# Pooled attention with a Strassen output product: when x is turned, which queue loads and stores, and which engine combines

## The chip, the cores and the metric

The kernel runs on one core of a Trainium2 chip. The metric is the device time of one execution in microseconds (us). A core has several engines that run side by side, each with its own instruction queue: TensorE (PE, matrix products), VectorE (DVE), ScalarE (ACT), GpSimd (POOL) and SyncE (SP), which here only issues transfers. Sixteen DMA engines move the data. A transfer is put on a queue by the engine that issues it: in the profile q1 is the queue of SP, q10 that of ACT, and q0 ("software_dynamic") that of POOL.

## The reference

Eight batches of eight heads, 576 queries each, head size 64; keys and values are pooled by eight to 72. The attention output, as a 4608 x 512 matrix x, goes through two products with a function between them.

```python
def _attn_ref(q, k, v):
    pool = 8
    k_p = k.reshape(B, H, S // pool, pool, D).mean(axis=3)
    v_p = v.reshape(B, H, S // pool, pool, D).mean(axis=3)
    scores = np.matmul(q, k_p.transpose(0, 1, 3, 2)) / np.sqrt(D)
    scores = scores - np.max(scores, axis=-1, keepdims=True)
    attn = np.exp(scores)
    attn = attn / (np.sum(attn, axis=-1, keepdims=True) + 1e-09)
    return np.matmul(attn, v_p)

x = attn_out.transpose(0, 2, 1, 3).reshape(4608, 512)
h = x @ w_in            # w_in  512 x 2048
g = h - np.tanh(h)
out = g @ w_out         # w_out 2048 x 512
```

## The kernel before

The two products are worked in nine groups of 512 tokens (`TG`, g = 0 to 8). A batch has 576 tokens, so the borders of batches and groups drift apart: group g + 1 needs only the first blocks of batch g + 1, and the rest of that batch is read by group g + 2. Group 0 and the attention of batches 0 and 1 are a start of their own. From g = 1 on the order is written out by hand (the schedule is manual: each engine runs its instructions in program order, and semaphores tie the engines together), and each group has two phases.

In the **h phase** (line 934 on) PE computes x @ w_in by `h_pair` and `h_one` (line 530, 62 to 64 matmuls with 512 columns), reading `xT`, a ring of three groups' columns. ACT takes tanh, DVE subtracts (L543, L548) and adds up the sums that Strassen's scheme needs (P at L551, Q at L556).

In the **output phase** (line 962 on) seven products of Strassen's scheme (L586, 16 matmuls of 256 columns each) stand in for the eight of a 2 x 2 block product. `after_product` combines them into O: L626 after product 1, then differences Dg (L561), L631 on GpSimd and L635 after products 2 and 3, L638 after 4, L640 after 5; ACT copies the last quarter at L983. Between the products stands the attention of the next batch nb = g + 1: scores (L349) in steps 0 to 4, and in steps 6, 7, 8, 9 and 11 the products with V, one block of 128 queries each (`av`, L396). A block has two halves; each is normalised by DVE with a reciprocal (L413) and a multiplication (L414) into `x_sb`, and the block is then turned into `xT` by a DMA transpose on SP's queue (L434; a block that crosses the ring's end takes two).

SP's queue in a group, in order: five or six transposes of x (L434), one of k (L332, from `kd`, which POOL makes), five of q (L205, from `q_bf`, which ACT casts in the first three steps of the h phase), then the nine loads of k, v and q of batch nn = g + 2 (L137, L146, L141, L170, L162).

POOL's queue in a group: L631, then pooling of k (L248, L253, L256) and v (L267 to L291) of batch nn, then `k_place` (L300 to L304, which needs the turned k), then the stores of the group before (L607, five to eight transfers).

After the last group's phase SP stores O (L603, eight transfers), two halves of the last product are copied out (L994) and stored on SP and ACT (L996).

```python
if by_dma:                                   # in av, after both halves
    nc.sync.dma_start_transpose(out=xT[...], in_=x_sb[...])
if nn is not None:                           # third step of the h phase
    load_k(nn); load_v(nn); load_q(nn)       # all on nc.sync
if u == 6 and nn is not None:
    pool_k(nn, nc.gpsimd)
    pool_v(nn, nc.gpsimd)
```

Of the kernel before, what the change touches and what calls it, by code (L numbers as in the profile page):

```python
# [8 lines left out]
FP32 = mybir.dt.float32  # L9
# [3 lines left out]
ALU = mybir.AluOpType  # L13
PSUM = bass.MemoryType.PSUM

B, H, S, D = 8, 8, 576, 64
# [10 lines left out]
TG = 512  # L27
# [15 lines left out]
def kernel(  # L43
# [89 lines left out]
            nc.vector.tensor_copy(out=out, in_=in_)  # L133
        evac_n[0] += 1

    def load_main(src, dst, b, t0, t1):
        return nc.sync.dma_start(out=dst[:, t0:t1, :], in_=src[b, 0:128, t0:t1, :])  # L137

    def load_left(src, dst, b, eng=nc.sync):
        return [  # L140
            eng.dma_start(out=dst[32 * t : 32 * t + LO, NM, :], in_=src[b, 128:PR, t, :])  # L141
            for t in range(NM)
        ]

    def load_dense(src, dst, b, eng=nc.sync):
        return eng.dma_start(  # L146
            out=dst[0 : NM * LO, NM, :], in_=src[b, 128:PR, :, :]
        )

    def load_k(b):  # L150
        return [
            load_main(k_pairs, k_raw[b % 2], b, 0, NM),
            load_dense(k_pairs, k_raw[b % 2], b),
        ]

    def load_v(b):
        return [load_main(v_pairs, v_raw[b % 2], b, 0, NM)] + load_left(
            v_pairs, v_raw[b % 2], b
        )

    def load_q_tail(b, t, eng):
# [1 line left out]
            out=t[:QT, :, R, :], in_=q[b, :, QA:S, :].rearrange("h p d -> p h d")  # L163
        )

    def load_q(b, tail=True):
        if b not in q_raws:
            q_raws[b] = raw.tile([128, H, R + 1, D], FP32, name="q_raw", tag="q_raw")
        t = q_raws[b]
        nc.sync.dma_start(  # L170
            out=t[:, :, 0:R, :], in_=q[b, :, 0:QA, :].rearrange("h (p j) d -> p h j d", j=R)
        )
        if tail:
            load_q_tail(b, t, nc.sync)

    qTs = {}
    kdups = {}
# [60 lines left out]
    def halves(n, b):  # L238
        return ((0, n),) if b < 2 else ((0, n // 2), (n // 2, n))

    def pool_k(b, eng, t0=0, t1=NT, mid=()):
        r = k_raw[b % 2].rearrange("p t (j d) -> p t j d", d=D)[:, t0:t1, :, :]
        if b not in kdups:
            kdups[b] = work.tile([128, NT, 2, D], BF16, name="kd", tag="kd")
        kd = kdups[b][:, t0:t1, :, :]
        n = t1 - t0
        for ta, tb in halves(n, b):
            first = eng.tensor_tensor(  # L248
                out=r[:, ta:tb, 0:4, :], in0=r[:, ta:tb, 0:4, :], in1=r[:, ta:tb, 4:8, :], op=ALU.add
            )  # L250
        for c in mid:
            load_w2(c)
        eng.tensor_tensor(  # L253
            out=r[:, :, 0:2, :], in0=r[:, :, 0:2, :], in1=r[:, :, 2:4, :], op=ALU.add
        )
        eng.tensor_tensor(  # L256
            out=kd,
            in0=r[:, :, 0:1, :].to_broadcast([128, n, 2, D]),
            in1=r[:, :, 1:2, :].to_broadcast([128, n, 2, D]),
            op=ALU.add,  # L260
        )
        return first
# [158 lines left out]
    def new_x():  # L421
        return work.tile([128, 2, 4, D], BF16, name="x_sb", tag="x_sb", bufs=5)

    def av(b, blk, alloc, by_dma):
        x_sb = new_x()
        for half in range(2):
            av_half(b, blk, half, x_sb, alloc)
        if by_dma:
            p0 = 0 if blk < 4 else 64
            pos = (b * S + blk * 128) % RING  # L430
            p1 = min(128, p0 + RING - pos)
            for r0, r1, c in ((p0, p1, pos), (p1, 128, 0)):
                if r1 > r0:
                    nc.sync.dma_start_transpose(  # L434
                        out=xT[:, :, c : c + r1 - r0],
                        in_=x_sb[r0:r1, :, :, :].rearrange("p a h d -> p (a h d)"),
                    )
        return x_sb

    def x_pe_transpose(b, blk, x_sb, fbs=(0, 4)):  # L440
        p0 = 0 if blk < 4 else 64
# [116 lines left out]
        )  # L558

    def sum_d(a, b):  # L560
        nc.vector.tensor_tensor(  # L561
            out=Dg[:, a:b, :, :],
            in0=Gt[:, a:b, :, 0:HT],
            in1=Gt[:, a:b, :, HT:TG],
            op=ALU.subtract,
        )
# [30 lines left out]
            return PS[:, 2:4, 0:HD]  # L597
        return PS[:, bk, :].rearrange("p (t n) -> p t n", t=2)

    def store(g, th, c0=0, c1=DM):  # L600
        for tt in range(2):
            for r0, r1, dst in out_segments(g * TG + th * HT + tt * 128, 128):
                nc.sync.dma_start(out=dst[:, c0:c1], in_=O[r0:r1, 2 * th + tt, c0:c1])  # L603

    def store_tile(g, tb):
        for r0, r1, dst in out_segments(g * TG + tb * 128, 128):
            nc.gpsimd.dma_start(out=dst, in_=O[r0:r1, tb, :])  # L607

    def sh(c, off):
        return slice(c.start + off, c.stop + off)  # L610
# [8 lines left out]
        (C1, lambda k, c: Dg[:, k, 1, c], w2s[:, 2, :, :]),  # L619
    ]  # L620

    def after_product(g, n):
        if n == 0:
            nc.scalar.copy(out=m4, in_=chain(g, C1))
        if n == 1:
            nc.vector.tensor_tensor(out=O[:, 2:4, 0:HD], in0=chain(g, C2), in1=m4, op=ALU.add)  # L626
            sum_d(0, 2)
            sum_d(2, 4)
        if n == 2:
            nc.scalar.copy(out=m45, in_=chain(g, C1))  # L630
            nc.gpsimd.tensor_tensor(out=m4, in0=O[:, 2:4, 0:HD], in1=m45, op=ALU.subtract)  # L631
            sum_d(4, 6)
            sum_d(6, 8)
        if n == 3:
            nc.vector.tensor_tensor(out=O[:, 0:2, HD:DM], in0=m4, in1=chain(g, C2), op=ALU.subtract)  # L635
        if n == 4:
            nc.scalar.copy(out=m451, in_=chain(g, C1))  # L637
            nc.vector.tensor_tensor(out=m451, in0=m451, in1=m45, op=ALU.subtract)  # L638
        if n == 5:
            nc.vector.tensor_tensor(  # L640
                out=O[:, 2:4, HD:DM], in0=m451, in1=chain(g, C2), op=ALU.subtract
            )
# [288 lines left out]
    for g in range(1, NG):  # L931
        nb = g + 1 if g + 1 < B else None
        nn = g + 2 if g + 2 < B else None
        for p in range(NP - 1):
            c = p if g > 1 else p - 1
            if nb is not None and 0 <= c < 3:
                q_cast_part(nb, c)
            h_pair(g, p, (0, 2, 4, 6, 0, 2, 4)[p], p % 2)
            if g == 1 and p < 4:
                w_sum(w2s[:, 0, :, :], b11, b22, ALU.add, k0=2 * p, k1=2 * p + 2)  # L940
            if 3 <= p < 6:
                sum_p(2 * p - 6, 2 * p - 4)
            if nb is not None and p == 0:
                k_dma_transpose(nb)
                k_place(nb, nc.gpsimd.tensor_copy)
            if g > 1 and p == 0:
                for tb in range(4):
                    store_tile(g - 1, tb)
            if nb is not None and 0 <= c < 3:
                q_dma_transpose(nb, 2 * c, min(2 * c + 2, R + 1))  # L950
            if nb is not None and c == 2:
                if nn is not None:
                    load_k(nn)
                    load_v(nn)
                    load_q(nn)
        h_one(g, NP - 1, 1, 0, 2)
        h_one(g, NP - 1, 0, 1, 3)
        sum_p(6, 8)
        sum_q(0, 4)
        sum_q(4, 8)  # L960
        ps_a = Banks(2, 3, 4, 5, 0, 1)
        for u in range(14):
            n, half = u // 2, u % 2
            bk, lhs, rhs = products[n]
            if n == 6 and g == NG - 1:
                break
            product(g, bk, lhs, rhs, 4 * half, 4 * half + 4, n < 2)
            if half:
                after_product(g, n)
                if g == 1 and n in (1, 2):  # L970
                    w_sum(w2s[:, 2, :, :], b21, b22, ALU.add, k0=4 * n - 4, k1=4 * n)
            if nb is not None:
                if u < NT:
                    scores(nb, u)
                if u == NT:
                    ps_a.n += 2
                if u in (6, 7, 8, 9, 11):
                    av(nb, (6, 7, 8, 9, 11).index(u), ps_b1, True)
                if u == 6 and nn is not None:
                    pool_k(nn, nc.gpsimd)  # L980
                    pool_v(nn, nc.gpsimd)
        if g < NG - 1:
            nc.scalar.copy(out=O[:, 0:2, 0:HD], in_=chain(g, C1))  # L983
    store(NG - 1, 1)
    store(NG - 1, 0, c0=HD)
    bk, lhs, rhs = products[6]
    for tt in range(2):
        product(NG - 1, bk, lhs, rhs, 0, NP, False, (tt,))
        for c0, c1, eng in (
            ((0, HD, nc.scalar.copy),)  # L990
            if tt == 0
            else ((0, HD // 2, nc.scalar.copy), (HD // 2, HD, nc.vector.tensor_copy))
        ):
            eng(out=O[:, tt, c0:c1], in_=part(NG - 1, C1, tt, c0, c1))  # L994
        for n, (r0, r1, dst) in enumerate(out_segments((NG - 1) * TG + tt * 128, 128)):
            (nc.sync, nc.scalar)[n % 2].dma_start(out=dst[:, 0:HD], in_=O[r0:r1, tt, 0:HD])  # L996


# [28 lines left out]
```

## Time and profile before

| | |
|---|---|
| median of 13 runs | 302.94 us (300.44 to 305.29) |
| the profiled execution's own time | 304.82 us |
| its span, first to last instruction | 303.1 us |
| TensorE clock granted, mean over the span | 0.987 |
| moved by DMA | 49.85 MB |
| q1 (SP), q0 (POOL), q10 (ACT): share of 16 DMA engines | 47.6%, 18.7%, 2.2% |
| POOL's idle time before L631, over 8 groups | 102.1 us |

The span is what the profile sees; the time of the execution is 1.72 us longer. The mean granted clock is below 1 mostly from one stretch, at about 182 to 197 us, where the table by stretches shows 0.89. In the views below, "idle before <- releaser" on an engine's line tells how long the engine stood still before that instruction and what ended it; a queue line such as "SPq" is the time in which the issuing engine was occupied with issuing, not the time of the transfer.

### The profile page before, as it was taken

The page shows a single profiled execution, that of the slowest core. Times are in us where ns is not written, and L with a number is a line of the kernel's source. Part 1 is how long each engine was busy: PE and PEld are TensorE (multiplying, and loading weights), DVE is VectorE, ACT ScalarE, POOL GpSimd, SP SyncE. Part 2 cuts the span into 40 slices and gives each one's busy share as a digit, 9 for nine tenths or more (in the row PEclk, how much of TensorE's full clock was granted, in tenths as well). Part 3 has the DMA queues.
Part 4 walks back from the last instruction along what each step waited for, and adds up shares of the span by engine and source line. Part 5 has one row for each costly group of instructions (what it writes and reads, how often), then busy time and mean ns, then how long its engine had stood idle before and what let it go on. Part 6 is the DMA issues. An engine that isn't in the chain of part 4 may idle for free.

```text
span 303.1 us, 5447 instructions
## 1 busy us (share of the span) xinstructions
PE 280.9 (93%) x2021; PEld 179.0 (59%) x2040; DVE 229.8 (76%) x400; ACT 154.1 (51%) x244; POOL 145.0 (48%) x166
## 2 busy tenths in 40 slices
PE   7899899999989898979999979999999999999980
PEld 3454356446854586448846864489447945864770
DVE  5658676799978878696959883899698949938950
ACT  4647676676247632855276425670766055135410
POOL 8500919950699149902994399109950140130010
PEclk9999999999999999999999997999999999999997
DMA  7999999749536996599949995993370350021014
GB/s 258 214 215 281 319 243 317 207 85 330 143 70 114 271 313 81 116 248 307 109 90 238 313 148 107 284 313 71 67 201 2 69 149 2 0 106 35 0 25 117
DMA packets 64588, 49.85 MB, mean 164 GB/s; under 512 B 39985, under 2 KB 53297, under 8 KB 64561
## 3 DMA queue, kind: packets, MB, share of 16 engines
q1 hardware_dynamic: 54736, 35.60, 47.6%
q0 software_dynamic: 7248, 12.06, 18.7%
q10 hardware_dynamic: 2576, 1.84, 2.2%
q8 instruction: 16, 0.26, 0.4%
q14 instruction: 12, 0.09, 0.1%
HBM read 36.70 MB, written 9.44 MB: 152 GB/s over the span
## 4 chain that ended last, share of the span: by engine, by line
PE 54%; DMA 19%; POOL 10%; DVE 7%; issue 4%; SPq 2%; ACT 1%; ACTq 0%; DVEq 0%; POOLq 0%
PE PS L530 24%; PE PS L586 21%; DMA w1b<-in_moe_w_in_dram 4%; DMA qT<-q_bf 4%; PE PS L512 4%; DMA k_raw<-in_k_dram 4%; DMA xT<-x_sb 3%; DVE Gt L543 3%; PE PS L396 2%; PE PS L349 2%; DMA v_raw<-in_v_dram 2%; POOL k_raw L248 2%; DMA out_dram<-O 2%; POOL out_dram L607 1%; POOL k_raw L253 1%
## 5 line engine op out<-in xcount | busy, mean ns | idle before, releaser
L530 PE MATMUL PS<-xT,w1b 128*128 128x512 bf16 x496 | 112.8, 383 | 5.9 <-DMA xT<-x_sb 4.3
L543 DVE TENSOR_TENSOR Gt<-PS,TS 128x1024 bf16<-128x1024 f32 x56 | 68.3, 1220 | 31.1 <-ACT TS L542 31.1
L530 PEld LDWEIGHTS <-w1b 128*128 128x128 f16 x512 | 50.2, 99 | 66.0 <-issue 6.6
L542 ACT ACTIVATE TS<-PS 128x1024 f32<-128x1024 f32 x56 | 57.4, 1025 | 37.0 <-PE PS L530 27.9
L631 POOL TENSOR_TENSOR m<-O,m 128x512 f32<-128x512 f32 x8 | 10.8, 1355 | 102.1 <-ACT m L630 55.4
L414 DVE TENSOR_TENSOR x_sb<-PS,rden 128x256 bf16<-128x256 f32 x72 | 30.5, 424 | 2.5
L586 PE MATMUL PS<-w2s,Dg 128*128 128x256 f16 x256 | 30.2, 273 | 0.0
L607 POOL DMA_DIRECT2D out_dram<-O x44 | 23.6, 546 | 13.4 <-ACT O L983 13.4
L248 POOL TENSOR_TENSOR k_raw<-k_raw 128x512 f32<-128x512 f32 (+2 forms) x13 | 22.0, 1711 | 16.4 <-DMA k_raw<-in_k_dram 16.4
L586 PEld LDWEIGHTS <-Gt 128*128 128x128 bf16 x256 | 24.4, 98 | 7.1 <-issue 1.4
L586 PEld LDWEIGHTS <-P 128*128 128x128 bf16 x256 | 24.6, 98 | 4.7 <-issue 1.4
L368 ACT ACTIVATE E<-PS 128x288 bf16<-128x288 f32 x60 | 21.7, 410 | 10.3 <-PE PS L349 10.1
L586 PEld LDWEIGHTS <-Dg 128*128 128x128 bf16 x256 | 24.6, 98 | 2.6
L561 DVE TENSOR_TENSOR Dg<-Gt 128x1024 bf16<-128x1024 bf16 x32 | 23.2, 782 | 0.0
L551 DVE TENSOR_TENSOR P<-Gt 128x1024 bf16<-128x1024 bf16 x32 | 21.9, 686 | 0.5
L349 PE MATMUL PS<-qT,KB 128*128 128x288 bf16 (+5 forms) x128 | 17.5, 289 | 3.1 <-DMA qT<-q_bf 2.9
L396 PE MATMUL PS<-VB,E 128*128 128x130 bf16 x240 | 20.2, 220 | 0.1
L637 ACT COPY m<-PS 128x512 f32<-128x512 f32 x8 | 4.7, 586 | 29.5 <-PE PS L586 29.5
L267 POOL TENSOR_TENSOR v_raw<-v_raw 128x512 f32<-128x512 f32 (+1 forms) x12 | 19.2, 1621 | 0.0
L396 PEld LDWEIGHTS <-E 128*128 128x128 bf16 x240 | 16.8, 98 | 1.9 <-issue 0.4
L586 PE MATMUL PS<-w2s,Gt 128*128 128x256 f16 x128 | 16.7, 273 | 0.4 <-DVE Gt L548 0.2
L983 ACT COPY O<-PS 128x512 f32<-128x512 f32 x7 | 4.1, 586 | 24.5 <-PE PS L586 24.5
(109 smaller groups left out, 399.8 us busy)
## 6 DMA issues: line engine op xcount, KB each, us to landing
k_raw<-in_k_dram SPq DMA_DIRECT2D x7, 1024.0 KB, 9.0
q_raw<-in_q_dram SPq DMA_DIRECT2D x7, 1024.0 KB, 11.2
v_raw<-in_v_dram SPq DMA_DIRECT2D x7, 1024.0 KB, 10.6
out_dram<-O POOLq DMA_DIRECT2D x32, 128.0 KB, 4.1
out_dram<-O POOLq DMA_DIRECT2D x12, 256.0 KB, 3.6
w1b<-in_moe_w_in_dram POOLq DMA_DIRECT2D x4, 512.0 KB, 14.1
w2b<-in_moe_w_out_dram POOLq DMA_DIRECT2D x4, 512.0 KB, 16.4
out_dram<-O SPq DMA_DIRECT2D x4, 256.0 KB, 4.0
```

The lines of the kernel that those rows point to most:

```text
L248: first = eng.tensor_tensor(out=r[:, ta:tb, 0:4, :], in0=r[:, ta:tb, 0:4, :], in1=r[:, ta:tb, 4:8, :], op=ALU.add)
L349: nc.tensor.matmul(dst[p : p + w], lhsT=KB[b % 2][:, o : o + w], rhs=qTs[b][:, m, c0:c1], start=True, stop=True,)
L368: nc.scalar.activation(out=E[:, t, half * hs : (half + 1) * hs], in_=ps[:, :], func=ACT.Exp, scale=SCALE)
L396: nc.tensor.matmul(ps[:, 2 * n : 2 * n + 2, :].rearrange("p h d -> p (h d)") if n < 2 else ps.rearrange("p (a s) d -> p a s d", s=2)[:, :, ...
L414: nc.vector.tensor_tensor(out=x_sb[:, half, :, :], in0=ps[:, :, 0:D], in1=rden[:, :, :].to_broadcast([128, 4, D]), op=ALU.mult,)
L530: nc.tensor.matmul(dst, lhsT=w1b[:, fb, i * 128 : (i + 1) * 128], rhs=xT[:, fb, c0 : c0 + TG], start=(fb == 0), stop=(fb == NFB - 1),)
L542: nc.scalar.activation(out=t2, in_=PS[:, b0 : b0 + 2, :], func=ACT.Tanh)
L543: nc.vector.tensor_sub(out=Gt[:, p, :, :], in0=PS[:, b0 : b0 + 2, :], in1=t2)
L551: nc.vector.tensor_tensor(out=P[:, a:b, :], in0=Gt[:, a:b, 0, :], in1=Gt[:, a:b, 1, :], op=ALU.add)
L561: nc.vector.tensor_tensor(out=Dg[:, a:b, :, :], in0=Gt[:, a:b, :, 0:HT], in1=Gt[:, a:b, :, HT:TG], op=ALU.subtract,)
L586: nc.tensor.matmul(part(g, bk, tt), lhsT=lhs(k, slice(tt * 128, (tt + 1) * 128)), rhs=rhs[:, k, :], start=(first and k == 0 and (tt == 0 o ...
L607: nc.gpsimd.dma_start(out=dst, in_=O[r0:r1, tb, :])
```

## The change

- In `av`, on the path by DMA, both halves of a block are normalised by one reciprocal and one multiplication (`av_both`), on the same two PSUM banks as before.
- A block is turned at once only where the next group reads it (the first 3, 3, 2, 2, 1, 1 blocks of batches 2 to 7). The others go on a list `late` and are turned at the begin of the next group's output phase.
- The nine loads of k, v and q in a group are issued by GpSimd, at the same place in the program; the stores of a finished group by SP: two row blocks in the first step of the h phase, between the turning of k and of q, two in the fourth, after q.
- L631 moves from GpSimd to VectorE, behind product 3's last matmul and the first block's normalisation; all four Dg differences follow product 1; the pooling of k waits for the last of them (`gate`).
- In the last group half of O's quarters are stored after product 3, the rest after product 5 on SP and GpSimd; the last two copies are one on ACT and one on DVE, and their stores three on ACT and one on SP.

PE's instructions and their order are unchanged. DVE has 274 rows of instructions in place of 328.

```diff
+    def av_both(b, blk, x_sb):
+        b0 = ps_a.ids[ps_a.n % len(ps_a.ids)]
+        ps_a.n += 2
+        ps = PS[:, b0 : b0 + 2, 0 : 4 * D1].rearrange("p k (h d) -> p k h d", d=D1)
+        for half in range(2):
+            av_mms(b, blk, half, ps[:, half, :, :])
+        rden = work.tile([128, 2, 4, 1], FP32, name="rden2", tag="rden2")
+        nc.vector.reciprocal(out=rden[:, :, :, :], in_=ps[:, :, :, D:D1])
+        nc.vector.tensor_tensor(out=x_sb[:, :, :, :], in0=ps[:, :, :, 0:D],
+            in1=rden[:, :, :, :].to_broadcast([128, 2, 4, D]), op=ALU.mult)
...
         if by_dma:
+            if b * S + blk * 128 < (b + 1) * TG:
+                x_dma_transpose(b, blk, x_sb)
+            else:
+                late.append((b, blk, x_sb))
...
     def store_tile(g, tb):
         for r0, r1, dst in out_segments(g * TG + tb * 128, 128):
-            nc.gpsimd.dma_start(out=dst, in_=O[r0:r1, tb, :])
+            nc.sync.dma_start(out=dst, in_=O[r0:r1, tb, :])
...
         if n == 1:
             nc.vector.tensor_tensor(out=O[:, 2:4, 0:HD], in0=chain(g, C2), in1=m4, op=ALU.add)
-            sum_d(0, 2)
-            sum_d(2, 4)
+            for k in range(0, NP, 2):
+                gate[0] = sum_d(k, k + 2)
         if n == 2:
             nc.scalar.copy(out=m45, in_=chain(g, C1))
-            nc.gpsimd.tensor_tensor(out=m4, in0=O[:, 2:4, 0:HD], in1=m45, op=ALU.subtract)
-            sum_d(4, 6)
-            sum_d(6, 8)
         if n == 3:
+            nc.vector.tensor_tensor(out=m4, in0=O[:, 2:4, 0:HD], in1=m45, op=ALU.subtract)
             nc.vector.tensor_tensor(out=O[:, 0:2, HD:DM], in0=m4, in1=chain(g, C2), op=ALU.subtract)
+            if g == NG - 1:
+                store(g, 1, (nc.sync, nc.sync), 0, HD)
+                store(g, 0, (nc.sync, nc.sync), HD, DM)
...
-            if g > 1 and p == 0:
-                for tb in range(4):
+            if g > 1 and p in (0, 3):
+                for tb in (2, 3) if p == 0 else (0, 1):
                     store_tile(g - 1, tb)
...
-                    load_k(nn)
-                    load_v(nn)
-                    load_q(nn)
+                    load_k(nn, nc.gpsimd)
+                    load_v(nn, nc.gpsimd)
+                    load_q(nn, eng=nc.gpsimd)
...
+        while late:
+            x_dma_transpose(*late.pop(0))
         ps_a = Banks(2, 3, 4, 5, 0, 1)
...
-                    pool_k(nn, nc.gpsimd)
+                    pool_k(nn, nc.gpsimd, dep=gate[0])
...
-    store(NG - 1, 1)
-    store(NG - 1, 0, c0=HD)
+    store(NG - 1, 1, (nc.sync, nc.gpsimd), HD, DM)
     bk, lhs, rhs = products[6]
-    for tt in range(2):
+    for tt, eng in ((0, nc.scalar.copy), (1, nc.vector.tensor_copy)):
         product(NG - 1, bk, lhs, rhs, 0, NP, False, (tt,))
...
+        eng(out=O[:, tt, 0:HD], in_=part(NG - 1, C1, tt))
         for n, (r0, r1, dst) in enumerate(out_segments((NG - 1) * TG + tt * 128, 128)):
-            (nc.sync, nc.scalar)[n % 2].dma_start(out=dst[:, 0:HD], in_=O[r0:r1, tt, 0:HD])
+            (nc.scalar if tt == 0 or n else nc.sync).dma_start(
+                out=dst[:, 0:HD], in_=O[r0:r1, tt, 0:HD]
+            )
```

## The prediction

> **What bounds the kernel now.** I read the page first, then PE's waits, PE's timeline at the phase borders, SP's timeline, and the last 10 us.
>
> ```profile
> span 303.1 us, 5447 instructions
> PE 280.9 (93%) x2021; PEld 179.0 (59%) x2040; DVE 229.8 (76%) x400; ACT 154.1 (51%) x244; POOL 145.0 (48%) x166
> ```
>
> PE is the bound. Its work is not touched, so only its 22 us of idle time can change: the start (not in the diff), the phase borders, and the end. In the table of waits two lines on PE come from transfers:
>
> ```profile
> PE PS L530 <- DMA xT<-x_sb: 4.3, 3, 2.1
> PE PS L349 <- DMA qT<-q_bf: 2.9, 3, 1.5
> ```
>
> PE's timeline places them (bracket: idle before, and what ended it):
>
> ```profile
> 87.22 13.99 PE L530 MATMUL PS<-xT,w1b 128*128 128x512 bf16 x62 [0.85 <-DMA xT<-x_sb]
> ...
> 103.41 0.28 PE L349 MATMUL PS<-qT,KB 128*128 128x288 bf16 x1 [1.21 <-DMA qT<-q_bf]
> ...
> 119.32 13.97 PE L530 MATMUL PS<-xT,w1b 128*128 128x512 bf16 x62 [1.34 <-DMA xT<-x_sb]
> ...
> 135.82 0.30 PE L349 MATMUL PS<-qT,KB 128*128 128x288 bf16 x1 [1.53 <-DMA qT<-q_bf]
> ...
> 181.75 15.66 PE L530 MATMUL PS<-xT,w1b 128*128 128x512 bf16 x62 [2.13 <-DMA xT<-x_sb]
> ```
>
> Groups 2, 3 and 5 start late for x (0.85 + 1.34 + 2.13 = 4.32), groups 2, 3 and 6 wait for q in their output phase (1.21 + 1.53 + 0.18 = 2.92): 7.24 us in all. Other borders are closed. SP's timeline of group 2's output phase and group 3's h phase shows why:
>
> ```profile
> 113.32 7.93 SPq L434 DMA_TRANSPOSE xT<-x_sb  x5
> 121.35 1.23 SPq L332 DMA_TRANSPOSE kT<-kd  x1
> 122.68 7.69 SPq L205 DMA_TRANSPOSE qT<-q_bf  x5
> 130.42 0.91 SPq L137 DMA_DIRECT2D k_raw<-in_k_dram  x1
> ```
>
> All is one serial queue: the q transposes come after five of x, and the loads after them, so late that they still move when the next x is turned. The timeline of the end:
>
> ```profile
> 292.83 0.69 DVE L640 TENSOR_TENSOR O<-m,PS 128x512 f32<-128x512 f32 x1 [0.44 <-PE PS L586]
> 293.55 5.46 SPq L603 DMA_DIRECT2D out_dram<-O  x8
> ...
> 294.76 0.27 ACT L994 COPY O<-PS 128x128 f32<-128x128 f32 x1 [0.68 <-PE PS L586]
> ...
> 299.11 1.17 SPq L996 DMA_DIRECT2D out_dram<-O  x2
> ```
>
> The last data are ready by 295.4, but their store waits for eight older ones on SP until 299.11.
>
> **What the Trainium skill says.** "SBUF — State Buffer", section "SBUF: two separate sides": VectorE and GpSimd share a port pair under an exclusive lock; a VectorE operation with two SBUF inputs waits for the whole GpSimd instruction. DVE's and POOL's timelines agree:
>
> ```profile
> 146.87 2.00 DVE L638 TENSOR_TENSOR m<-m,m 128x512 f32<-128x512 f32 x1
> ...
> 176.09 2.00 DVE L638 TENSOR_TENSOR m<-m,m 128x512 f32<-128x512 f32 x1
> ```
>
> The same operation takes 0.69 in the last group, where POOL is idle; at 146.87 it ends 0.55 after POOL's L253 (146.78 to 148.32). The same section warns that a DMA from GpSimd's queue needs that port for its descriptors; here L607 kept to 527 to 598 ns in all 44 issues with DVE busy beside it, so I see no such stall. "DMA: Bandwidth & Descriptors", section "Issuing engines are not separate DMA queues": whichever engine issues, transfers share the 16 DMA engines; another issuer saves issuing time only. The trace fits: q transposes waited up to 7.9 us to land (median 2.5) with loads and stores of two queues in flight.
>
> **The change part by part.**
>
> *The end.* L626 of the last group is done at 286.7, so four stores go out during product 2; L635, done before at 290.8, is about 0.8 earlier, because the Dg differences (3.56 us there, 2.5 without POOL's L631 between them) are not held up; four more leave SP at 290.0 to 292.6 at 0.59 to 0.65 each. After L640 (293.5) SP has two, POOL two (0.54 each, landing 2.3 to 4.1 later, so by about 298.2). The last copy is one 128x256 on DVE, some 0.42 from 294.76 (L414 takes 0.42 for 256 columns from PSUM), and its stores leave at about 295.3. Before, the last issue began at 299.7 and the span ended 3.4 later; 295.3 + 3.4 = 298.7. Gain 4.4; the POOL stores could hold it to 3.9. I take 4.3.
>
> *q.* Let h be the start of the h phase, and I the issue of the last x transpose needed: h = I + 2.6 (landing 2.47 plus 0.14). Then on SP: 1.2 for it, 1.25 for k (its `kd` is ready at about the same time as before, 118.5 in place of 118.7), two or four stores at 0.6, and five q transposes at 1.3. The last q transpose is issued at I + 8.9 or I + 10.1, that is h + 6.3 or h + 7.5; before it was 129.1 - 119.3 = h + 9.8. It is needed at h + 15.0 (102.2 - 87.2). So it may take 7.5 to 8.7 us to land, against 7.9 at most before. It is crowded as before: POOL ends `k_place` at h + 7.5 (126.9), and in place of 1 MB of stores now starts the loads there. The moved stores cost SP 1.2 to 2.4 us ahead of q, more than covered by the two to four x transposes (about 1.2 to 1.6 each) taken out. Bounds: all 2.92 gained, or none. I take 2.4.
>
> *Loads on POOL.* Nine issues per group: six at 0.54 (L607), three large ones at 0.75 to 1.0 (L656, L727): 5.5 to 6.2 us, in POOL's idle 9.5 to 16 us ahead of L631. The q load also waits for ACT's last cast at about h + 5.5, already past. They start at h + 7.5 in place of h + 11 and end at h + 13.5 in place of h + 20, hence are further from the next x transposes. If the cover were gone, `pool_k` and then k's transpose would be late by the excess.
>
> *x.* One reciprocal and one 0.69 multiplication (L816 is this form: 691 ns) replace two of each (four times 0.2 to 0.34): 0.25 less per block, 1.2 per group. Against this L631 adds 0.69 to DVE, and it lands under POOL's pooling, which now starts right at the gate: L248's two parts take 1.26 and 1.8. The new subtraction arrives about 0.9 to 1.4 after the gate; it either slips between the two parts (0.55 after a wait up to 0.5) or waits out the second (up to 2.4 in all). So the second and third blocks come from 0.7 earlier to 2 later. By group: 1 to 2, with `w_sum` also in the crossfire, I put the gap at 1.75 for 0.85 (-0.9); 2 to 3: third block at 115.4 for 116.1, +0.5; 3 to 4, closed now, two blocks: 0 to 0.9 lost, -0.3; 4 to 5: same issue time or up to 2 later, but landing nearer to 3 than to the 6.65 that the chain of waits shows at 174.96, +1.0. Groups 6 and 7 need one block only. Sum +0.3, between -3 and +4.3. The late blocks cost SP 2.5 to 6 us at the begin of the output phase, where it is free until the first block at about 8 us after.
>
> **Sum.** 4.3 + 2.4 + 0.3 = 7.0. On the profiled execution: span 303.1 to 296.1, time 304.82 to 297.8. That execution is 1.9 over the median, about what its one stretch of 0.89 clock costs (15.66 for 13.98 on the line at 181.75). Taken from the median: 302.94 - 7.0 = 295.9.
>
> **Rivals.**
> - *Only the end.* x and q waits stay at 7.2 because the lock delays blocks and POOL's loads crowd q: 302.94 - 4.3 = 298.6. For: the lock's 2.00 lines. Against: q's three-microsecond head start.
> - *All gone.* 302.94 - 4.3 - 7.24 = 291.4. For: fewer transposes in the way. Against: DVE's order leaves the third block hardly earlier.
> - *Slower.* Loads on POOL's queue overlap the last q transposes in all six attention groups. q is issued at h + 6.9 on average and needed at h + 15.0: each microsecond of landing over 8.1 costs six. It eats the other gains (4.3 + 2.92 + 0.3 = 7.5) from 9.4 us on; at the 10.6 us that v's loads take (median), six times 2.5 is 15, giving 310.4. For: 7.9 was seen. Against: that was with as much in flight.
> - *It doesn't arrive:* gains and new waits cancel, 302.9.
>
> **Chances.** Forecast 0.50 (own range 293.3 to 298), only the end 0.20, all gone 0.15, slower 0.10, cancel 0.05. What one measurement can tell from no change is about 0.5%, 1.5 us. Faster 0.85, within 0.05, slower 0.10. The range 291.0 to 299.5 leaves out about 0.15 to 0.2.
>
> **What would show it.** The last issue on SP and ACT near 295.3 of an otherwise equal timeline (shifted by the gains). No line of PE's wait for qT above 0.3, SP's q transposes over by h + 8. The x waits near 1.7, 0.8, 0.3 and 1.1 at the starts of groups 2 to 5. The subtraction on DVE at 0.69 in the last two groups and 0.6 to 2.5 before. Nine POOL issues of 5.5 to 6.2 in each h phase. The forecast is wrong if q lands later than 9 us after issue, if POOL's issues take twice as long, or if the clock is granted less for longer once PE's gaps close.

## The result and the profile after

| | median of the runs | ratio to before, 95% interval |
|---|---|---|
| before | 302.05 us (298.52 to 307.13, 48 runs) | |
| after | 319.18 us (314.43 to 320.79, 11 runs) | 1.0521 [1.0473, 1.0569] |

The change makes the kernel slower: the medians differ by 17 us, and the ratio, which takes only the executions within 1.5% of the fastest one of each kernel, gives 15.7. The profiled execution of after took 320.79 us, its span 318.7, against 304.82 and 303.1 before, each above the median of its kernel: 15.6 us of span to explain. The page's head, with the busy time of each engine:

```profile
span 318.7 us, 5363 instructions
PE 285.2 (89%) x2021; PEld 181.0 (57%) x2040; DVE 230.5 (72%) x348; ACT 153.9 (48%) x243; POOL 142.8 (45%) x161
```

PE executes the same 2021 matmuls, yet is busy for 4.3 us longer (285.2 for 280.9) and idle for 11.3 longer. DVE executes 348 instructions, where it had 400. PE's waits (line, what it waited for: us in all, times, longest):

```profile
PE PS L351 <- DMA qT<-q_bf: 16.0, 4, 8.7
PE PS L614 <- DVE O L663: 2.8, 5, 1.2
...
PE PS L558 <- DVE x_sb L434: 1.5, 1, 1.5
...
PE PS L558 <- DMA xT<-x_sb: 0.7, 1, 0.7
```

The wait for the turned q was 2.9 us and is 16.0; the second line is new. PE's timeline shows where (the bracket is the idle time before):

```profile
88.34 13.97 PE L558 MATMUL PS<-xT,w1b 128*128 128x512 bf16 x62 [0.69 <-DMA xT<-x_sb]
...
112.75 0.42 PE L351 MATMUL PS<-qT,KB 128*128 128x288 bf16 x1 [8.71 <-DMA qT<-q_bf]
112.96 1.92 PE L614 MATMUL PS<-w2s,Gt 128*128 128x256 f16 x8
...
131.39 13.97 PE L558 MATMUL PS<-xT,w1b 128*128 128x512 bf16 x62 [1.50 <-DVE x_sb L434]
...
148.66 0.30 PE L351 MATMUL PS<-qT,KB 128*128 128x288 bf16 x1 [2.30 <-DMA qT<-q_bf]
...
181.57 0.33 PE L351 MATMUL PS<-qT,KB 128*128 128x288 bf16 x1 [2.94 <-DMA qT<-q_bf]
...
215.85 0.42 PE L351 MATMUL PS<-qT,KB 128*128 128x288 bf16 x1 [2.04 <-DMA qT<-q_bf]
...
247.18 0.41 PE L351 MATMUL PS<-qT,KB 128*128 128x288 bf16 x2
```

Groups 2 to 5 wait at the start of their attention, 8.71 + 2.30 + 2.94 + 2.04 = 16.0. Group 6 doesn't, and it is the one attention group in which no batch is left to load: a control that the kernel carries in itself. Group 1 is a second one. It has loads and doesn't wait, but its loads start when SP is at the last of q's five transposes:

```profile
59.68 6.41 SPq L205 DMA_TRANSPOSE qT<-q_bf  x5
```

```profile
65.10 0.80 POOL L137 DMA_DIRECT2D k_raw<-in_k_dram  x1
```

The chain that ended last, cut at group 2, names the transfer (start, us, what):

```profile
97.17 0.22 ACT TS L570
97.38 15.32 DMA qT<-q_bf
112.70 0.05 issue
```

The last q transpose was issued at 97.38 and landed (its data had arrived) 15.3 us later. What the DMA engines did meanwhile is in the view of the DMA queues. First from 101 to 108 us (packets, MB, share of the 16 engines):

```profile
DMA packets 976, 1.65 MB, mean 236 GB/s; under 512 B 570, under 2 KB 570, under 8 KB 976
...
q0 software_dynamic: 487, 1.53, 80.2%
q1 hardware_dynamic: 489, 0.12, 12.7%
```

and from 111 to 113 us:

```profile
DMA packets 595, 0.59 MB, mean 295 GB/s; under 512 B 351, under 2 KB 351, under 8 KB 595
...
q1 hardware_dynamic: 573, 0.54, 90.7%
q0 software_dynamic: 22, 0.05, 8.0%
```

q0 carries GpSimd's loads, q1 what SP issues. In the seven microseconds both queues get as many packets, 487 and 489; but a packet of q0 moved 3.1 KB on average and one of q1 0.25 KB, so the loads got 93% of the bytes. In the two microseconds in which the loads run dry, q1 passes 573 packets (stores of O among them, 0.54 MB in all), four times as many in a microsecond. Turning q takes about 2,400 such small packets (0.58 MB in the view of a1 below), a batch's loads 1,040 packets (3.54 MB, q0 from 94 to 113 us). Here the two queues look served in turn, packet for packet. From 97 to 111 us q0 passes 979 packets and q1 1,275: in 14 us little more than half of what q's turning needs, so the turning ends when the loads do. The load of q, issued at 98.51, took 13.4 us, so it landed at 111.9; q's last transpose landed at 112.7. The counts are not equal in every stretch: from 99 to 101 us they are 172 of q0 and 335 of q1, and from 207 to 211 us, with a transpose of q in flight, 302 and 95.

Before, SP issued the loads behind the transposes of q, on the same queue. The trace of after shows how far they have come forward, on SP and on POOL (start, us, engine, line, x how many):

```profile
91.93 6.69 SPq L205 DMA_TRANSPOSE qT<-q_bf  x5
98.67 2.64 SPq L635 DMA_DIRECT2D out_dram<-O  x4
```

```profile
94.44 0.81 POOL L137 DMA_DIRECT2D k_raw<-in_k_dram  x1
...
98.51 0.96 POOL L170 DMA_DIRECT2D q_raw<-in_q_dram  x1
```

In group 2 the loads start at 94.44, with most of the five q transposes still to be issued. In groups 3 to 5 they start later against q (136.68, 170.62 and 205.20, with q's issue from 132.14 to 140.05, 166.54 to 173.12, and 200.90 to 207.34), so that only q's last transposes fall among them. These take 9.7 to 10.7 us to land, and PE's waits are 2 to 3 us.

**The account of the 15.6 us.** Waits for q: 16.0 for 2.9, +13.1. Waits for L663: +2.8. PE slower while busy: +4.3. Waits for x: 2.6 (0.69 + 1.50 + 0.44) for 4.3, -1.7. From PE's last matmul to the span's end: 4.67 (318.7 - 310.37 - 3.66) for 8.56, -3.9. The sum is 14.6; 1.0 is in small waits that I do not assign.

Most of the 4.3 us come with the waits. Eight matmuls of L614 take 1.92 us at 112.96, right after the longest wait, and 1.04 at 117.11. The table by stretches (busy us of PE, PEld, DVE, ACT, POOL with counts; then granted clock, DMA share, GB/s):

```profile
104.00:113.00 9.00, 0.29 (x3) 0.17 (x3) 2.13 (x4) 0.41 (x1) 0.00 (x0) 0.65 1.08 258
113.00:117.00 4.00, 4.00 (x21) 2.80 (x20) 0.00 (x0) 1.61 (x4) 0.00 (x0) 0.52 0.26 40
117.00:121.00 4.00, 4.00 (x43) 3.17 (x41) 2.76 (x5) 2.50 (x7) 0.00 (x0) 1.00 0.00 0
...
180.00:192.00 12.00, 10.43 (x89) 8.32 (x90) 6.12 (x11) 4.33 (x11) 2.02 (x2) 0.86 0.99 236
...
214.00:225.00 11.00, 9.15 (x75) 7.12 (x76) 6.02 (x12) 4.59 (x12) 0.76 (x1) 0.84 0.98 266
```

After 8.71 idle us PE gets half its clock for another 4 us: some 1.9 us (4 x 0.48) on top of the wait. The stretches at 180 and 214 hold the waits of groups 4 and 5; what their clocks lack is 1.7 (12 x 0.14) and 1.8 us (11 x 0.16) at most. Before, apart from the end, there was one such stretch, of 1.7 us. So 5.4 for 1.7, or up to 3.7 of the 4.3. Not every wait does it: after the 2.30 us of group 3 the clock stays at 1.00.

### The profile page after: what moved, and what is told of

Read it like the earlier page. It is cut to its first block, busy times and chain, and to the rows that moved or that the text cites. A ratio compares the mean times of both kernels' runs of the same rounds, so it can differ in the third digit from the quotient of the medians.

```text
span 318.7 us, 5363 instructions
## 1 busy us (share of the span) xinstructions
PE 285.2 (89%) x2021; PEld 181.0 (57%) x2040; DVE 230.5 (72%) x348; ACT 153.9 (48%) x243; POOL 142.8 (45%) x161
## 4 chain that ended last, share of the span: by engine, by line
PE 52%; DMA 15%; DVE 3%; issue 2%; ACT 0%
PE PS L614 25%; PE PS L558 22%; DMA qT<-q_bf 14%; PE PS L351 2%; PE PS L398 2%; DVE m L669 1%; DMA xT<-x_sb 1%; DVE x_sb L434 1%; DVE O L663 1%; DVE rden L433 1%; ACT TS L570 0%; DVE O L671 0%; DVE O L1021 0%
## 5 line engine op out<-in xcount | busy, mean ns | idle before, releaser
L558 PE MATMUL PS<-xT,w1b 128*128 128x512 bf16 x496 | 111.1, 379 | 4.5 <-DVE x_sb L434 1.5
L248 POOL TENSOR_TENSOR k_raw<-k_raw 128x512 f32<-128x512 f32 (+2 forms) x13 | 21.9, 1698 | 75.3 <-DVE Dg L589 58.3
L631 POOL DMA_DIRECT2D out_dram<-O x2 | 1.1, 574 | 73.8 <-DVE O L671 73.8
L351 PE MATMUL PS<-qT,KB 128*128 128x288 bf16 (+5 forms) x128 | 18.8, 299 | 16.7 <-DMA qT<-q_bf 16.0
L614 PE MATMUL PS<-w2s,Dg 128*128 128x256 f16 x256 | 30.2, 272 | 2.8 <-DVE O L663 2.8
L614 PEld LDWEIGHTS <-Gt 128*128 128x128 bf16 x256 | 25.6, 102 | 6.7 <-DVE Gt L576 0.5
L614 PEld LDWEIGHTS <-P 128*128 128x128 bf16 x256 | 25.7, 102 | 5.9 <-issue 1.4
L614 PEld LDWEIGHTS <-Dg 128*128 128x128 bf16 x256 | 24.7, 98 | 6.1 <-issue 3.5
L656 DVE TENSOR_TENSOR O<-PS,m 128x512 f32<-128x512 f32 x8 | 5.5, 688 | 25.3 <-ACT E L370 25.0
L434 DVE TENSOR_TENSOR x_sb<-PS,rden 128x512 bf16<-128x512 f32 x30 | 20.7, 691 | 1.0
L269 POOL TENSOR_TENSOR v_raw<-v_raw 128x512 f32<-128x512 f32 (+1 forms) x12 | 21.5, 1809 | 0.0
L351 PEld LDWEIGHTS <-KB 128*128 128x128 bf16 (+1 forms) x128 | 7.4, 99 | 22.0 <-DMA qT<-q_bf 17.1
L589 DVE TENSOR_TENSOR Dg<-Gt 128x1024 bf16<-128x1024 bf16 x32 | 19.9, 682 | 0.0
L614 PE MATMUL PS<-w2s,Gt 128*128 128x256 f16 x128 | 19.3, 301 | 0.4 <-DVE Gt L576 0.2
L614 PE MATMUL PS<-w2b,P 128*128 128x256 f16 x128 | 18.2, 293 | 0.0
```

Of the source, the lines that this page charges most:

```text
L248: first = eng.tensor_tensor(out=r[:, ta:tb, 0:4, :], in0=r[:, ta:tb, 0:4, :], in1=r[:, ta:tb, 4:8, :], op=ALU.add)
L269: eng.tensor_tensor(out=r[:, ta:tb, 0:4, :], in0=r[:, ta:tb, 0:4, :], in1=r[:, ta:tb, 4:8, :], op=ALU.add)
L351: nc.tensor.matmul(dst[p : p + w], lhsT=KB[b % 2][:, o : o + w], rhs=qTs[b][:, m, c0:c1], start=True, stop=True,)
L434: nc.vector.tensor_tensor(out=x_sb[:, :, :, :], in0=ps[:, :, :, 0:D], in1=rden[:, :, :, :].to_broadcast([128, 2, 4, D]), op=ALU.mult,)
L558: nc.tensor.matmul(dst, lhsT=w1b[:, fb, i * 128 : (i + 1) * 128], rhs=xT[:, fb, c0 : c0 + TG], start=(fb == 0), stop=(fb == NFB - 1),)
L589: return nc.vector.tensor_tensor(out=Dg[:, a:b, :, :], in0=Gt[:, a:b, :, 0:HT], in1=Gt[:, a:b, :, HT:TG], op=ALU.subtract,)
```

## The experiments

All ratios are to the kernel before, run on the same chip beside it. a2 and b1 have no ratio: their four executions lie too far apart for one.

| kernel | us, median (range, runs) | ratio, interval |
|---|---|---|
| a1: after, loads on SP | 298.22 (297.13 to 299.9, 4) | 0.9858 [0.9786, 0.993] |
| a2: after, stores on GpSimd | 307.79 (302.18 to 340.66, 4) | |
| a3: after, loads held until q is turned | 307.61 (305.67 to 309.79, 4) | 1.0165 [1.0081, 1.0249] |
| a4: after, loads on ACT | 369.98 (368.32 to 371.07, 4) | 1.2212 [1.2117, 1.2307] |
| b1: before, loads on GpSimd | 307.67 (304.91 to 310.29, 4), before 301.84 | |
| b2: after, only k on GpSimd | 297.83 (297.77 to 298.62, 4) | 0.9889 [0.9842, 0.9935] |
| b3: before, late x transposes alone | 299.45 (298.27 to 301.92, 22) | 0.9939 [0.9917, 0.9961] |
| b4: a1, stores ahead of loads, subtraction early | 298.85 (297.31 to 300.38, 10) | 0.9929 [0.9896, 0.9961] |
| c1: b2, subtraction early | 295.35 (294.28 to 296.45, 6) | 0.9806 [0.975, 0.9862] |
| c2: a1, subtraction early | 298.65 (297.58 to 301.42, 20) | 0.9926 [0.9901, 0.995] |
| c3: before, the change's end alone | 300.0 (297.54 to 307.11, 20) | 0.9928 [0.9898, 0.9959] |

My theory: the loads' own queue lets their packets alternate with those of q's transposes. The rivals: the stores on SP ahead of q make it late; the loads only come too early, on whatever queue; or any second queue does the same.

**a1, the loads back on SP, all else as after.**

```diff
-                    load_k(nn, nc.gpsimd); load_v(nn, nc.gpsimd)
-                    load_q(nn, eng=nc.gpsimd)
+                    load_k(nn); load_v(nn); load_q(nn)
```

> The changed kernel with its nine loads per group back on SP's queue, behind the q transposes. Theory (loads on a second queue share the DMA engines with the q transposes in flight): PE's wait for qT falls from 16.0 us to under 2, the slow clock after the long waits goes with it, and the time is 293 to 298 us, below before (302). Rival 1 (stores put ahead of and behind q on SP's queue delay it): the qT waits stay above 8 us and the time above 310. Rival 2 (the late x transposes crowd the q transposes): the same, above 310.

298.22, 21 us less than after and just above the expected range, with no wait for qT at all. PE's busy time falls with the waits, from 285.2 to 281.2 us. The time from the issue of q's transposes to their landing, from the views of after and of a1:

```profile
DMA to landing us min/median/max: 2.3/2.5/16.6
```

```profile
DMA to landing us min/median/max: 2.3/2.5/4.1
```

a1's DMA queues from 92 to 98 us, q's turning alone:

```profile
DMA packets 2415, 0.58 MB, mean 96 GB/s; under 512 B 2415, under 2 KB 2415, under 8 KB 2415
...
q1 hardware_dynamic: 2415, 0.58, 49.4%
```

The same kind of packets, five times as many in 6 us as the 489 in 7 us of after. Stores on SP ahead of q and the late transposes of x are in a1 too, so they are not the cause. What stays is a wait of PE for L663, 4.6 us in four places, and DVE's timeline says what delays L663:

```profile
114.03 0.69 DVE L663 TENSOR_TENSOR O<-m,PS 128x512 f32<-128x512 f32 x1 [2.28 <-DMA out_dram<-O]
```

L663 writes O over rows whose store still waits on SP behind the loads.

**a2, the stores on GpSimd, ahead of its loads.**

```diff
-            nc.sync.dma_start(out=dst, in_=O[r0:r1, tb, :])
+            nc.gpsimd.dma_start(out=dst, in_=O[r0:r1, tb, :])
-            if g > 1 and p in (0, 3):
-                for tb in (2, 3) if p == 0 else (0, 1):
+            if g > 1 and p == 0:
+                for tb in range(4):
```

> The changed kernel with its stores back on GpSimd's queue, all four row blocks in the first step of the h phase, ahead of the loads; loads stay on GpSimd. Theory (loads against q): the loads start about 3 us later, behind the stores, so the qT waits shrink but stay, 6 to 14 us, and the time is 308 to 318. Rival 1 (stores on SP's queue delay q): qT waits under 3 us, time 294 to 300.

The four executions took 302.18, 307.53, 308.05 and 340.66 us. The profile is that of the longest, where the waits for qT are 25.7 us and those for xT 11.5; it says nothing of the other three. Stores that delay the loads on GpSimd seem to help (three runs of four lie 6 us or more under every run of after), but the spread leaves the size open.

**a3, the loads on GpSimd, but issued only when q's last transpose has landed.**

```diff
+                    lds = load_k(nn, nc.gpsimd) + load_v(nn, nc.gpsimd)
+                    lds += load_q(nn, eng=nc.gpsimd)
+                    after(lds, q_last[0])
```

> The changed kernel, loads still on GpSimd's queue, but each waits until the last q transpose has landed. Theory (loads against q in flight): qT waits under 1 us; the loads then meet the x transposes, so x waits at the h phase grow to some us; time 294 to 302. Rival 1 or 2 (stores or late x transposes delay q): qT waits above 8 us, time above 310. A rival in which GpSimd's queue moves the loads more slowly as such: pooling of k late, waits of GpSimd on k_raw in each group.

No wait for qT is left (longest landing 3.0 us), as the theory has it. But the time is above what I expected: the loads now fall on the transposes of x. PE's waits, and its timeline at the start of one group:

```profile
PE PS L563 <- DMA xT<-x_sb: 7.1, 3, 3.3
```

```profile
120.76 0.58 PE L563 MATMUL PS<-xT,w1b 128*128 128x512 bf16 x1 [3.27 <-DMA xT<-x_sb]
```

x took up to 18.5 us to land: the loads on GpSimd's queue delay whichever transposes they meet. Ahead of this wait, from 106 to 112 us, the view of the DMA queues shows 477 packets of q0 (1.49 MB) and 475 of q1 (0.11 MB), again one for one. "Too early" is then no full account. In this group a3's loads start at 99.11 on GpSimd's queue and are in the way, while a1's, issued from 97.21 on by SP, hold up neither q nor x. The third forecast, that GpSimd's pooling would wait for k in each group, did not come: outside the start its pooling never waits for a load.

**a4, the loads on ACT's queue.**

```diff
-                    load_k(nn, nc.gpsimd); load_v(nn, nc.gpsimd)
-                    load_q(nn, eng=nc.gpsimd)
+                    load_k(nn, nc.scalar); load_v(nn, nc.scalar)
+                    load_q(nn, eng=nc.scalar)
```

> The changed kernel with its loads on ACT's queue at the same place of the program. If it is a second queue beside SP's that matters, whoever writes its descriptors: qT waits as in the changed kernel, 8 to 18 us, time 310 to 322. If it is a matter of descriptors written by GpSimd: qT waits under 3 us, and the time is 296 to 302, with about 5 us of issuing on ACT per group hidden or not in the h phase.

369.98, for another reason. ACT's timeline:

```profile
103.93 0.44 ACTq L137 DMA_DIRECT2D k_raw<-in_k_dram  x1
...
111.41 0.58 ACTq L146 DMA_DIRECT2D k_raw<-in_k_dram  x1
...
120.76 0.61 ACTq L162 DMA_DIRECT2D q_raw<-in_q_dram  x1
121.47 1.94 ACT L570 ACTIVATE TS<-PS 128x1024 f32<-128x1024 f32 x2 [17.25 <-DMA v_raw<-in_v_dram]
```

ACT stands idle for 17.25 us before its next tanh, 62 us in four such places, and PE then waits for ACT and DVE, not for q. So the time settles nothing about a second queue of ACT's kind. The trace gives a sign that it delays the transposes too: in this group, with k's load on ACT's queue beside them, q's transposes landed after 5.0 us in the median and 6.5 at most, in a1's after 2.4 and 2.5. Of the rivals, a1 rules out the first and a3 the second; whether any second queue would do as much harm as GpSimd's stays open.

**b1, before with nothing changed but the loads' queue.**

```diff
-                    load_k(nn); load_v(nn); load_q(nn)
+                    load_k(nn, nc.gpsimd); load_v(nn, nc.gpsimd)
+                    load_q(nn, eng=nc.gpsimd)
```

> The kernel before with one edit: its nine loads per group on GpSimd's queue, at the same place of the program (there they come after the stores of the finished group). Theory (DMA engines take packets from two queues in turn, one of 4096 bytes from the loads for one of 256 bytes from a transpose, so a transpose crawls while loads move): q or x transposes land 10 us and more after issue, PE waits for DMA qT or xT grow from 7.2 to over 15 us in all, the time is 308 to 325. Rival (the harm needs the changed order of transposes and stores): time within 300 to 305, waits as before.

The medians differ by 5.8 us. All four executions lie above 29 of the 31 of before, so the edit costs time here too, but how much is open: they spread over 5.4 us, and in the trace PE's waits for q and x together are 8.6 us (6.0 + 2.6), only 1.4 more than before. In after the edit costs far more. PE's waits for q:

```profile
PE PS L349 <- DMA qT<-q_bf: 6.0, 2, 5.3
```

Two waits in place of four: in before the stores stand ahead of the loads on GpSimd's queue, so that the loads start 2.8 to 4.2 us later (the time that issuing the stores takes in groups 2 to 4), when less of q is pending. In group 2 they start at 98.93, after SP's last issue for q (done at 97.70), and PE doesn't wait; in group 3 at 126.94, before it (128.78), and PE waits 5.34 us. So the cost follows how much of q's turning the loads overlap. I had expected waits of over 15 us.

**b2, only k on GpSimd, v and q on SP.**

```diff
-                    load_v(nn, nc.gpsimd); load_q(nn, eng=nc.gpsimd)
+                    load_v(nn); load_q(nn)
```

> The changed kernel with only the load of k on GpSimd's queue; v and q are loaded on SP's. Theory (packet for packet): a third of the packets of 4096 bytes, 288 instead of 832 a group, so a q transpose loses at most about 3 to 4 us, which the slack of some 3 us mostly hides: qT waits under 5 us in all and time 296 to 302. A theory in which any use of GpSimd's queue stalls the transposes: qT waits stay above 10 us, time above 310.

297.83, with 0.4 us of wait for q, as expected. q's longest landing is still 8.8 us, but with a third of the loads on the second queue PE waits for it only once. Against a1 (0.9858) no gain is shown.

**b3 and c3, two parts of the change alone, on before.** b3 has the late transposes of x only:

```diff
+            if b * S + blk * 128 < (b + 1) * TG: x_dma_transpose(b, blk, x_sb)
+            else: late.append((b, blk, x_sb))
...
+        while late: x_dma_transpose(*late.pop(0))
```

> The kernel before with one edit: blocks of x that the next group does not read are turned at the begin of the following output phase. What is said of the change's first part: x waits of 4.3 us and q waits of 2.9 us shrink to under 3 us in all, time 297 to 300 for 302. If that part does nothing: 301 to 303.

299.45. The waits for q vanish from PE's table, of those for xT 0.9 us is left (4.3 before), and a wait for a reciprocal of x (L413), 3.6, is in their place. So the part by itself does what it says, and hands part of it back to DVE's order. c3 has the end only: stores after product 3 on SP, the rest on SP and GpSimd, the last copies on ACT and DVE.

```diff
+    store(NG - 1, 1, (nc.sync, nc.gpsimd), HD, DM)
+    for tt, eng in ((0, nc.scalar.copy), (1, nc.vector.tensor_copy)):
+        (nc.scalar if tt == 0 or n else nc.sync).dma_start(out=dst[:, 0:HD], in_=O[r0:r1, tt, 0:HD])
```

> The kernel before with the change's end alone: half of O's quarters of the last group stored after product 3, the rest on SP and GpSimd, the last copies one on ACT and one on DVE. Theory: the last issue comes about 4 us earlier, time 297 to 299. If something else ends the span: 301 to 303.

300.0, by the ratio 0.0072 under before [0.0041, 0.0102], which is 2.2 us (1.2 to 3.1), about half of what I expected. In its trace the end after PE's last matmul is 5.7 us (296.5 - 287.13 - 3.66), 2.9 less than in before.

**b4, c1 and c2, for a version that beats both.** The subtraction L662 is put right behind the Dg differences, so that L663 waits for neither POOL's pooling nor it, and the pooling's `gate` is set on it; in b4 the stores of rows 0 and 1 also go ahead of the loads on SP.

```diff
-                gate[0] = sum_d(k, k + 2)
+                sum_d(k, k + 2)
         if n == 2:
+            gate[0] = nc.vector.tensor_tensor(
+                out=m4, in0=O[:, 2:4, 0:HD], in1=m45, op=ALU.subtract)
```

> The changed kernel with three edits: loads back on SP's queue; the stores of row blocks 0 and 1 on SP ahead of these loads; the subtraction that moved to VectorE put right behind the Dg differences, with GpSimd's pooling of k waiting for it. Theory: no qT wait, and the waits of PE on VectorE's L663 (4.6 us with loads on SP, where it waits for a store queued behind the loads) fall under 1 us: 292 to 296. If the subtraction or the store order doesn't matter: 297 to 299, as with the loads on SP alone.

298.85, no better than a1. PE's waits for L663 are gone, as expected, but the loads, pushed back to 103 to 110 us by the stores, now meet the transposes of x, which land after up to 9.0 us, and group 3 starts late:

```profile
122.39 0.59 PE L558 MATMUL PS<-xT,w1b 128*128 128x512 bf16 x1 [4.90 <-DMA xT<-x_sb]
```

c2 is a1 with the subtraction early, c1 is b2 with it:

> The changed kernel with all loads on SP's queue and the subtraction right behind the Dg differences; stores as in the changed kernel. L663 there also waited for stores behind the loads, so PE's waits on it shrink but one stays: 295 to 299. If the 4.9 us x wait of the version with the stores ahead of the loads came from the later loads, no x wait above 2 us here.

> The changed kernel with v and q loaded on SP's queue (k stays on GpSimd's), and the subtraction right behind the Dg differences, with the pooling of k waiting for it. If the waits of PE on L663 (2.9 us with k alone on GpSimd) come from the subtraction queueing behind GpSimd's pooling, they fall under 0.5 us and the time is 294 to 296.5. If not: 297 to 299 as with k alone.

c2 has no wait of PE for x above 1.0 us, so b4's 4.9 did come with its later loads. But c2 gains nothing over a1: DVE's waits show L665 (L663 in after) held by the store that sits behind the loads on SP.

```profile
DVE O L665 <- DMA out_dram<-O: 11.1, 4, 4.5
```

c1 takes k off SP, and with it that store comes earlier: these waits of DVE fall from 11.1 to 5.0 us. PE's waits for both former culprits:

```profile
PE PS L351 <- DMA qT<-q_bf: 1.9, 1, 1.9
...
PE PS L614 <- DVE O L665: 0.3, 1, 0.3
```

295.35, 0.9806 [0.975, 0.9862]: the lowest median of all, clearly ahead of c2 on the same chip; its interval still overlaps those of a1 and b2, so a lead over these two is not shown.

## Why the prediction was wrong, point by point

- **The step that failed is *q*.** "So it may take 7.5 to 8.7 us to land, against 7.9 at most before. It is crowded as before: POOL ends `k_place` at h + 7.5 (126.9), and in place of 1 MB of stores now starts the loads there." I counted what was in flight as bytes on shared engines. Before, the second queue held 1 MB of stores, and the 3.5 MB of loads stood behind q on q's own queue. After, 3.5 MB come on the other queue beside q's small packets, and q landed after up to 16.6 us where the step allowed 7.5 to 8.7. a1 undoes this step alone, and 21 us go. A smaller part of the step was off too: in group 2 the last q transpose was issued at h + 9.0 (97.38 - 88.34), not h + 7.5, not least because SP spent 3.45 us on the four stores ahead of q and not 2.4.
- **What I read in the Trainium skill.** From "DMA: Bandwidth & Descriptors", section "Issuing engines are not separate DMA queues", I took that another issuer saves issuing time only. The same page, section "SWDGE vs HWDGE vs iDMA", has what decides: inside each DMA engine the queues of the two kinds (GpSimd's, and those of SP and ACT) are served in turn, and an engine switches at packet boundaries. The trace agrees from 101 to 108 us, with 487 to 489 packets; it doesn't from 207 to 211 us, where q1 got fewer still (95 to 302). I should have priced the transposes in packets.
- **The rival *Slower*** had the right place, a threshold (9.4 us of landing) that was passed, and a wait in all of 15 against 16.0 measured. That the sums are so close is luck: it reckoned six equal waits of 2.5 us from the median landing of v's loads, and there were four, one of them 8.7; only five of the six groups have loads. Its 310.4 lacks the two terms below. Its chance of 0.10 was too small: that the 7.9 of before "was with as much in flight" was the same mistake.
- **A term that is in no case: the clock.** The sum let only PE's idle time change. But its busy time rose by 4.3 us, most of it where the waits are, down to a granted clock of 0.52; with the waits gone in a1, 4.0 of it go too.
- **A second missing term: product 5's wait for L663.** I worked out that the moved subtraction would land under POOL's pooling, and only asked what this costs the blocks of x. That PE waits for L663 to read a PSUM bank before it can write there cost 2.8 us.
- **The subtraction itself** was right. DVE's and POOL's timelines of after:

```profile
122.78 2.29 DVE L662 TENSOR_TENSOR m<-O,m 128x512 f32<-128x512 f32 x1
...
308.55 0.68 DVE L662 TENSOR_TENSOR m<-O,m 128x512 f32<-128x512 f32 x1
```

```profile
121.48 3.03 POOL L248 TENSOR_TENSOR k_raw<-k_raw 128x512 f32<-128x512 f32 x2 [19.74 <-DVE Dg L589]
```

  2.29 beside POOL's L248, 0.68 without, where 0.6 to 2.5 and 0.69 were forecast.
- ***Loads on POOL*:** 0.81 + 0.54 + 0.78 + 1.99 + 0.96 + 0.71 = 5.8 us, as forecast (5.5 to 6.2). They start 6.1 us after h (94.44 - 88.34), earlier than the 7.5 that I took, which made the collision worse.
- ***x*:** waits of 0.69, 1.50, 0 and 0.44 at groups 2 to 5, where 1.75, 0.85, 0.3 and 1.1 stood: 2.6 in all for 4.0, better than forecast.
- ***The end*:** 3.9 us gained in after, 4.3 forecast. SP's last issue is at 314.52, 0.49 after the end of PE's last matmul (314.03), and ACT's issues are over at 315.89; before, SP's last was at 299.7, 5.2 after. Alone (c3) it brought 2.2 us by the ratio of times.

With the loads on SP the rest of the change comes near the 295.9: a1 has 298.22, and 4.6 us of wait for L663 in it that the sum did not have.

## What to carry to other kernels

A queue is also an order: moving large transfers from the queue on which they stood behind something urgent to one of their own lets them run beside it, and in this kernel the queue with the small packets (the DMA transposes) then lost: with as many packets as the other queue, it moved a twelfth of the bytes. So count packets, not bytes, and ask of every transfer that changes queue which small-packet transfer it stood behind, and when that one is needed. Stores behind loads on one queue hold up whoever writes their buffer next; here a third of the loads on the other queue (c1: PE waits 1.9 us for q and 0.3 for L665) was faster than none (c2: nothing for q, 4.5 for L665).

## What the runs showed of the hardware that was not expected

- For 7 us two DMA queues with packets of very different size got one packet each: 487 to 489, 1.53 MB to 0.12 MB; in a3 for 6 us, 477 to 475. Without loads beside them, 2415 of the small ones passed in 6 us.
- After a wait of 8.71 us PE's granted clock was 0.52 for 4 us, then 1.00 again.
- Loads issued from ACT made ACT stand for 7.5 us between the first issue (103.93) and the second (111.41), and 17.25 us before its next activation.
- Still open: in b2, from 126 to 129 us, the queue view shows 171 packets of q0 and none of q1, though a q transpose issued at 124.94 was pending and landed 8.79 us later. In after, from 207 to 211 us, it shows 302 to 95. One for one doesn't explain these stretches, in which q1 gets less than its turn; no run was made on them.
